# Attention and capacity-limited experts on one core: joined rows of the last tile, an earlier next-to-last scatter, expert counts copied to SBUF with later placements

## The chip, the cores and the metric

One core of one Trainium2 chip. The metric is device time in microseconds of one execution of the whole kernel. A profiled execution gives the trace, from which all rows below come.

## The reference

Causal attention over 8 batches, 12 heads, 448 positions and head width 64; its output, 3584 rows of 768, goes to a top-1 expert layer with 8 experts, at most 80 tokens each (those with the largest gate weight).

```python
scores = scale * np.matmul(q, k.transpose(0, 1, 3, 2))
scores = np.where(mask, -1000000000.0, scores)              # mask: above the diagonal
attn = np.exp(scores - np.max(scores, axis=-1, keepdims=True))
attn = attn / (np.sum(attn, axis=-1, keepdims=True) + 1e-09)
x = np.matmul(attn, v)                                      # then (B*S, H*D): 3584 x 768
...
logits = x @ w_gate
expert_idx = np.argmax(logits, axis=1)
gate_w = probs[np.arange(N), expert_idx]                    # softmax of the logits
for e in range(E):
    tok_idx = np.where(expert_idx == e)[0]
    if len(tok_idx) > capacity:                             # capacity 80
        tok_idx = tok_idx[np.argpartition(-gate_w[tok_idx], capacity)[:capacity]]
    h = np.maximum(x[tok_idx] @ w1[e], 0.0)
    out[tok_idx] = gate_w[tok_idx, None] * (h @ w2[e])
```

## The kernel before

**Attention.** The loop goes over 48 pairs of heads, six per batch, each in 8 slots. The order of instructions on every engine is the order in which the program emits them; nothing reorders it. In one pair's turn TensorE does the corner scores of this pair (L547), transposes the exponentials of the pair before (L597, four groups of four blocks, each in one bank of PSUM out of four that rotate under the tag "g"), multiplies the flipped exponentials of the pair before that with the values (L620), and starts the scores of the next pair (L540). VectorE adds the mask and finds the minimum (L559, `ns`, `nb`), ScalarE takes the exponential (L563), and ScalarE (three groups) and VectorE (the fourth) copy the transposes to the flipped buffer `PT` (L602). The product `xp` is copied to `xu`, one column per query, by ScalarE (L629). The four tiles of 448 queries are three of 128 (t = 0 to 2, queries 64 to 447) and one of 64 (t = 3, the first 64 queries in memory; the code calls it the last tile).

**Steps of a batch.** What a finished batch still needs is spread over the pairs of the next one and a bit further by a table of slots: `later_on` puts a step at `ends` + slot, so slots 0 to 7 fall in pair 0 of the next batch, 16 to 23 in its pair 2, 48 to 55 in pair 0 of the batch after it. `STEPS` has the slots for most batches, `EARLY` those of the next-to-last batch.
- `norms`: `guard`, `invert` and `last_rows` turn the sums of the softmax into their reciprocals; `last_rows` gathers those of the last tile into `rl`.
- `row_group(t, g)`: for tile t and three pairs of heads (g = 0 or 1), three transposes of `xu` (L731), one multiply by the reciprocals (L750), one store to the scratch rows `xs` (L755). `ROWS0` and `ROWS1` have their slots.
- `gate_products` (L681), `gate_rows` and `gate`: logits of the experts.
- `select_groups`: keeps a table of the 80 largest weights of each expert over the batches so far. `rl`, `lt`, `cp` count how many of a batch's tokens are larger than each kept one (`cp`, L908, a bank of PSUM), `places` and `places2` (L928, VectorE, half the experts each) turn the counts into one-hot rows `rm`, `c0` to `c3` compare tokens with each other (L879, L882), `earlier` (GpSimd, `rank`, L968), `own`, `rank` and `rr` make the new tokens' places, `tn` (L1015, L1021) moves the table.

**Tail.** The last batch has no later pair to hide in; its steps stand in the string `TAIL`, which is executed from left to right: `r0w`, `r0e`, `r0m` are the transposes, the copy and the scaling of row group 0 and so on; an engine letter in `ROW_ENGINES` says who scales it ("p": ScalarE copies and GpSimd scales, "a": ScalarE scales). `*25` is 25 matmuls on constants (L1313) whose result nobody reads; they stand between the new table (`tn tab`) and the first expert.

**Experts.** `plan_experts` simulates the engines with a table of costs and returns an order of all steps. TensorE's own order is fixed in it: layer 1 and 2 of the experts alternate, one chunk of 128 inputs at a time ("p"), with "xtp" (transposes of gathered rows, L1374) and "ytp" (transposes of an expert's output, L1478) placed between chunks. `yo` scales the transposed output (L1488, L1490) and GpSimd scatters it to `out` by an indirect DMA (L1491); each scatter waits for the landing of the one before. The first three gathers (L1358) are issued before the first expert, and need the rows stored to `xs`.

Of the kernel before, what the change touches and what calls it, by code (L numbers as in the profile page):

```python
# [17 lines left out]
P = 128  # L18
# [9 lines left out]
ROWS0 = [(2, 2), (3, 4), (9, 9), (19, 20)]  # L28
ROWS1 = [(27, 28), (35, 36), (36, 38), (40, 41)]
STEPS = {'gp': 20, 'gs': 22, 'lp': 24, 'lg': 25, 'logit': 26, 'shifted': 27, 'chosen': 32, 'sums': 33, 'one_hot': 33, 'columns': 33, 'weight': 35, 'weighted': 36, 'parts': 37, 'r0t': 41, 'r0c': 42, 'r1t': 42, 'r1c': 43, 'rl': 44, 'lt': 46, 'c3w': 49, 'c3l': 50, 'cp': 53, 'ro': 53, 'places': 54, 'c2w': 56, 'c2l': 57, 'places2': 54, 'c1w': 58, 'c1l': 59, 'c0w': 60, 'c0l': 61, 'earlier': 61, 'gt': 65, 'own': 67, 'rank': 67, 'rr': 68, 'tn': 73, 'tab': 74, 'rp': 76, 'row': 78}  # L30
# [23 lines left out]
def plan_experts(E, layers, blocks, order, whole, pieces, loaded, buffers, his, los, ready_h, ready_l):  # L54

    pe = [("xtp", 0), ("warm", 0)]
    for e, w in layers:
        for x, c in enumerate(order[e, w]):
            n = len(order[e, w])
            if w == 1 and x == n // 2 and e == 0 and E > 1:  # L60
                pe.append(("xtp", 1))
            if x == (n // 2 if w == 1 else 3) and (e >= 2 if w == 1 else e == E - 1 and e > 0):
                pe.append(("ytp", e - 2 if w == 1 else e - 1))
            if w == 2 and x == n // 2 and e + 2 < E:
                pe.append(("xtp", e + 2))
            pe.append(("p", e, w, c))
# [107 lines left out]
def attention_then_moe(  # L174
# [91 lines left out]
    def whole_tile(t):  # L266

        return slice(queries(t).start, queries(t).start + P)
# [23 lines left out]
    for t in flipped:  # L292
        nc.vector.memset(part_of(t, slice(QB, P), COL[0], [WPT, 2], [COL[1] - COL[0], 2], [1, QB]), 0.0)
        nc.vector.memset(part_of(t, slice(0, QB), COL[2], [WPT, 2], [COL[3] - COL[2], 2], [1, QB]), 0.0)
# [274 lines left out]
    def transpose_groups(pr, n):  # L569

        pr.PT = flipped[n % 2]

        full = lambda t, j, at: pr.P[:, OFF[t, j] + at * QB:OFF[t, j] + at * QB + P]
# [6 lines left out]
        ways = [  # L580
            [(slice(0, P), 0, [[256, 2], [1, 256]], COL[0] + QB, [[WPT, 2], [1, 256]])],
            [(slice(0, P), 0, [[256, 2], [1, 256]], COL[1] + QB, [[WPT, 2], [1, 256]])],
            [(slice(0, P), 0, [[256, 2], [P, 2], [1, P]], COL[0] + S - P,
              [[WPT, 2], [COL[3] - P - (COL[0] + S - P), 2], [1, P]])],
            [(hi, QB, [[256, 2], [P, 2], [1, QB]], COL[2], [[COL[3] - COL[2], 2], [WPT, 2], [1, QB]]),
             (lo, QB, [[P, 2], [1, QB]], COL[1], [[WPT, 2], [1, QB]]),
             (lo, 256, [[QB, 2], [1, QB]], COL[0], [[WPT, 2], [1, QB]])],
        ]
# [46 lines left out]
    def norms(bt, ps):  # L635
# [28 lines left out]
        return [guard, invert, last_rows]  # L664

    def norm_of(bt, t, hs, m):
        return bt.rl[0:m, hs] if t == NO else bt.sums[0:m, t * H + hs.start:t * H + hs.stop]

    def gate_products(bt, which):
# [3 lines left out]
        def products(js=(0, 1), whole=range(NT)):  # L675
            if 0 in js:
                got[:] = [bank([P, len(which) * P], F32, "gp")]
            for x, i in enumerate(which):
                for j in js:
                    for t in whole:  # L680
                        nc.tensor.matmul(got[0][t * 4 * E:(t + 1) * 4 * E, x * P:(x + 1) * P], wgd[:, 2 * i + j, :],  # L681
                                         bt.xu[:, 2 * i + j, whole_tile(t)], start=(j == 0), stop=(j == 1))
# [33 lines left out]
    def row_group(bt, t, g, how="v"):  # L716

        b = bt.b
        m = min(P, S - t * P)
        got = []  # L720

        def turn():
# [7 lines left out]
            for i in range(NH):  # L730
                nc.tensor.transpose(tp[:, i, :], bt.xu[:, g * NH + i, whole_tile(t)], ident)  # L731

        def store():
# [5 lines left out]
            src = tp[0:m].rearrange("k p (j d) -> k (p j) d", d=DH)  # L739
            dst = xr[0:m].rearrange("k (h d) -> k h d", d=DH)  # L740
            norm = norm_of(bt, t, slice(g * 2 * NH, (g + 1) * 2 * NH), m)
# [7 lines left out]
            else:  # L749
                nc.vector.tensor_tensor(out=dst, in0=src, in1=norm.unsqueeze(2).to_broadcast([m, 2 * NH, DH]), op=ALU.mult)  # L750
            write(xr)

        def write(xr):
            r0 = b * S + queries(t).start
            nc.sync.dma_start(xs[r0:r0 + m, g * NH * P:(g + 1) * NH * P], xr[0:m, :])  # L755

        def scaled():
            _, (xr, dst, norm) = got
            nc.gpsimd.tensor_tensor(out=dst, in0=dst, in1=norm.unsqueeze(2).to_broadcast([m, 2 * NH, DH]), op=ALU.mult)
# [65 lines left out]
    def select_groups(bt):  # L825
# [61 lines left out]
        def table_chunk(s):  # L887
# [222 lines left out]
    def batch_plan(bt):  # L1110
# [4 lines left out]
        for g, rows in enumerate((ROWS0, ROWS1)):  # L1115
            for t in range(NT):
# [197 lines left out]
    for i, x in enumerate(ROW_ENGINES):  # L1314
        g, t = divmod(i, NT)
        steps.update(zip((f"r{i}w", f"r{i}e", f"r{i}m"), row_group(bt, t, g, x)))
# [264 lines left out]
```

## Time and profile before

| | us |
|---|---|
| median of 3 runs (lowest, highest) | 448.84 (448.57, 449.16) |
| profiled execution, its own time | 448.39 |
| its span, first to last instruction | 446.7 |

The span is the profiled time without 1.69 us around the first and the last instruction. A line of the trace gives the engine (PE TensorE, PEld its weight loads, DVE VectorE, ACT ScalarE, POOL GpSimd, SP SyncE), the line of the program, the operation, and what it writes and reads.

### The profile page before, as it was taken

How to read it: one execution, taken by the hardware profiler on the slowest of the kernel's cores; microseconds unless marked ns; L12 is line 12 of the kernel's file. 1: busy time of each engine (PE TensorE's matmuls, PEld its weight loads, DVE VectorE, ACT ScalarE, POOL GpSimd, SP SyncE). 2: the span in 40 equal slices, each digit the busy share in tenths (PEclk: the TensorE clock that was granted, in tenths of full speed). 3: DMA queues.
4: the chain of work that ended last, by engine and by line, in shares of the span. 5: the costliest groups of instructions: out<-in, count | busy, mean ns of one | idle time of the engine just before them, and what ended most of it. 6: DMA issues, size and time to landing. Idle time of an engine off the chain costs nothing. (4 is left out here: it accounts for less than half of the span.)

```text
span 446.7 us, 15791 instructions
## 1 busy us (share of the span) xinstructions
PE 427.3 (96%) x5830; PEld 331.0 (74%) x5830; DVE 383.2 (86%) x1315; ACT 391.3 (88%) x1069; POOL 241.5 (54%) x360
## 2 busy tenths in 40 slices
PE   8899999999999999999999999999899999899993
PEld 3576777777677777767766776765559999899992
DVE  6886698979879997987998889788879999989991
ACT  5999999989889988988989898878878999899971
POOL 7987728538665852856685384512561176415521
PEclk9999999999999999999999999999989999999998
DMA  7486769869686874866774354388479999999501
GB/s 228 140 283 213 237 209 322 256 215 307 233 266 203 290 236 139 306 232 230 243 244 151 98 181 148 135 298 307 161 247 346 401 414 400 397 415 412 229 26 45
DMA packets 47822, 109.95 MB, mean 246 GB/s; under 512 B 5970, under 2 KB 24402, under 8 KB 47104
## 3 DMA queue, kind: packets, MB, share of 16 engines
q1 hardware_dynamic: 46544, 105.20, 67.8%
q0 software_dynamic: 1056, 3.51, 2.4%
q8 instruction: 46, 0.75, 0.7%
q14 instruction: 32, 0.26, 0.2%
q10 hardware_dynamic: 144, 0.23, 0.2%
HBM read 85.35 MB, written 23.99 MB: 245 GB/s over the span
## 5 line engine op out<-in xcount | busy, mean ns | idle before, releaser
L563 ACT ACTIVATE prob<-ns,nb 128x192 f32<-128x192 f32 (+3 forms) x336 | 175.5, 532 | 17.6 <-DVE nb L559 16.1
L559 DVE CUSTOM_DVE_ANT_0 ns<-sp,mask 128x192 f32<-128x192 f32 (+3 forms) x336 | 134.4, 443 | 22.8 <-PE sp L540 21.1
L597 PE MATMUL tp<-ident,prob 128*128 128x128 f32 x768 | 104.4, 276 | 0.1
L1158 DVE SCALAR_TENSOR_TENSOR wl<-wraw,wh 128x768 f16<-128x768 f32 (+1 forms) x99 | 98.4, 1062 | 1.9 <-POOL wl L1507 1.6
L488 POOL TENSOR_TENSOR qk<-qk,qk 128x448 f16<-128x448 f32 x94 | 96.8, 1045 | 4.2 <-DVE qk L516 1.0
L620 PE MATMUL xp<-PT,vt 128*64 128x448 f32 (+3 forms) x768 | 93.6, 386 | 0.4 <-ACT PT L602 0.2
L1152 ACT ACTIVATE wh<-wraw 128x768 f16<-128x768 f32 (+1 forms) x99 | 86.5, 939 | 8.4 <-PE hp L1446 6.0
L597 PEld LDWEIGHTS tp<-ident,prob 128*128 128x128 f32 x768 | 84.2, 141 | 2.4 <-ACT PT L602 0.5
L620 PEld LDWEIGHTS xp<-PT,vt 128*64 128x64 f32 x768 | 50.8, 136 | 45.0 <-issue 24.5
L602 ACT COPY PT<-tp 128x512 f32<-128x512 f32 x144 | 76.3, 589 | 6.3 <-PE tp L597 5.8
L540 PE MATMUL sp<-qk 64*128 64x448 f16 (+2 forms) x864 | 69.2, 299 | 2.1 <-POOL qk L488 1.2
L1447 PEld LDWEIGHTS <-wl 128*128 128x128 f16 x678 | 67.7, 100 | 1.5 <-issue 1.4
L1446 PEld LDWEIGHTS <-wh 128*128 128x128 f16 x678 | 67.7, 100 | 1.1 <-issue 1.0
L1445 PEld LDWEIGHTS <-wh 128*128 128x128 f16 x678 | 68.2, 101 | 0.1
L563 ACT ACTIVATION_READ_ACCUMULATOR prob<-ns,nb 128x1 f32 x336 | 66.1, 197 | 0.0
L1491 POOL DMA_INDIRECT out<-yo,idx x8 | 36.8, 4602 | 51.7 <-ACT yo L1488 46.8
L540 PEld LDWEIGHTS <-qk 64*128 64x128 f16 x864 | 36.7, 95 | 17.4 <-issue 2.5
L602 DVE COPY PT<-tp 64x256 f32<-64x256 f32 x144 | 43.6, 327 | 2.3
L1447 PE MATMUL hp<-xh,wl 128*128 128x80 f16 x336 | 37.8, 202 | 1.4 <-issue 1.4
L1446 PE MATMUL hp<-xl,wh 128*128 128x80 f16 x336 | 37.7, 202 | 0.4 <-DVE xl L1390 0.4
L1445 PE MATMUL hp<-xh,wh 128*128 128x80 f16 x336 | 37.9, 202 | 0.0
L1446 PE MATMUL op<-hl,wh 128*128 128x80 f16 x318 | 36.3, 202 | 0.5 <-issue 0.4
(187 smaller groups left out, 658.9 us busy)
## 6 DMA issues: line engine op xcount, KB each, us to landing
wraw<-w SPq DMA_DIRECT2D x49, 384.0 KB, 8.6
wraw<-w SPq DMA_DIRECT2D x29, 512.0 KB, 9.1
out<-mask SPq DMA_DIRECT2D x56, 192.0 KB, 4.2
qk<-k_t SPq DMA_DIRECT2D x23, 448.0 KB, 4.6
qk<-q_t SPq DMA_DIRECT2D x23, 448.0 KB, 5.7
vt<-v_t SPq DMA_DIRECT2D x24, 384.0 KB, 6.1
xs<-xr SPq DMA_DIRECT2D x42, 192.0 KB, 2.8
wraw<-w SPq DMA_DIRECT2D x24, 256.0 KB, 4.3
```

Of the source, the lines that this page charges most:

```text
L488: sub = lambda e, o, a, b: e.tensor_tensor(out=o, in0=a, in1=b, op=ALU.subtract)
L540: nc.tensor.matmul(pr.sp[t, j], a[rows, p, queries(t)], c[rows, p, FROM[t]:FROM[t] + WIDTH[t]], start=(x == 0), stop=(x == 2))
L559: nc.vector.tensor_tensor_reduce(out=ns, in0=pr.sp[x], in1=m, scale=-1.0 / 8.0, scalar=HUGE, op0=ALU.add, op1=ALU.min, accum_out=nb)
L563: nc.scalar.activation(pr.P[:, OFF[x]:OFF[x] + w], got[0], AF.Exp, bias=got[1], scale=-1.0, accum_out=pr.sums[:, h:h + 1])
L597: nc.tensor.transpose(tp[:, i * P:(i + 1) * P], f, ident)
L602: way(part_of(pr.PT, rows, to, *todims), part_of(got[0], rows, at, *dims))
L620: nc.tensor.matmul(xp[rows, c * P:S], st["vt"][:, c, p * P + j * DH:p * P + (j + 1) * DH], pr.PT[:, j, n0:n0 + w], start=(c == 0), stop=(c ...
L1152: nc.scalar.activation(hi_of[y][:, 0:src.shape[1]], src, AF.Copy, scale=SW)
L1158: nc.vector.scalar_tensor_tensor(out=lo_of[y][:, 0:n], in0=src, scalar=SW, in1=hi_of[y][:, 0:n], op0=ALU.mult, op1=ALU.subtract)
L1445: nc.tensor.matmul(o, wh[:, ws], h[:, c, :], start=begin, stop=False, skip_group_check=True)
L1446: nc.tensor.matmul(o, wh[:, ws], l[:, c, :], start=False, stop=False, skip_group_check=True)
L1447: nc.tensor.matmul(o, wl[:, ws], h[:, c, :], start=False, stop=end, skip_group_check=True)
```

## The change

Five edits in one.
1. Pairs of heads with an even number keep their last tile at columns 384 to 447 of `xu` and not at 0 to 63. The last tile of an even pair and of the odd pair after it then lie side by side, and one transpose of 128 columns turns both. For tile 3 there is one row group in place of two: three transposes, one multiply over 128 partitions by a new array of reciprocals `rc`, and two stores, each of 64 rows with three pieces of 512 bytes a row. `rc` is filled by four more small copies on GpSimd per batch. The layouts of `PT`, of the products and of the gate products follow. In the last batch row group 3 and its steps leave `TAIL`, and row group 7 has the joined form.
2. "ytp" of the next-to-last expert stands before the third chunk of the last layer and not before the fourth.
3. `ro`, which did nothing, copies the counts `cp` to SBUF on ScalarE (all batches but the last), in `STEPS` one slot later; the placements read the copy.
4. In `STEPS`, `places` goes from slot 54 to 62 and `places2` from 54 to 68.
5. The matmuls before the first expert are 28 and not 25.

```diff
-ROWS0 = [(2, 2), (3, 4), (9, 9), (19, 20)]
+ROWS0 = [(2, 2), (3, 4), (9, 9)]
 ROWS1 = [(27, 28), (35, 36), (36, 38), (40, 41)]
...
-STEPS = {..., 'cp': 53, 'ro': 53, 'places': 54, ..., 'places2': 54, ...}
+STEPS = {..., 'cp': 53, 'ro': 54, 'places': 62, ..., 'places2': 68, ...}
...
-lp lg r1m rest rest logit r2w shifted r2e rest chosen rest r3w r3e *4
-sums one_hot columns r0t r0c r4w r4e *1 weight weighted parts hold rl r5w r5e r1t r1c *2 r3m r4m
+lp lg r1m rest rest logit r2w shifted r2e rest chosen rest *4
+sums one_hot columns r0t r0c r4w r4e *1 weight weighted parts hold rl r5w r5e r1t r1c *2 r4m
...
-gt1 c0l gt0 earlier own *5 rank rr tn tab *25
+gt1 c0l gt0 earlier own *5 rank rr tn tab *28
...
-            if x == (n // 2 if w == 1 else 3) and (e >= 2 if w == 1 else e == E - 1 and e > 0):
+            if x == (n // 2 if w == 1 else 2) and (e >= 2 if w == 1 else e == E - 1 and e > 0):
...
+    BEFORE = [QB, 0]
+    HEAD = [S - QB, 0]
+
+    def tile_of(bt, p, t):
+
+        at = p * S + (HEAD[p % 2] if t == NT - 1 else queries(t).start - BEFORE[p % 2])
+        return bt.xu.rearrange("k p s -> k (p s)")[:, at:at + P]
...
+                to = c * P - BEFORE[pr.p % 2] if c else 0
...
-                        xp[rows, c * P:S], st["vt"][:, c, p * P + j * DH:p * P + (j + 1) * DH],
+                        xp[rows, to:to + w], st["vt"][:, c, p * P + j * DH:p * P + (j + 1) * DH],
...
+                bt.rc = spool.tile([P, H // 2], F32, name="rqc", tag="rqc")
...
+            for x in range(2):
+                for j in range(2):
+                    nc.gpsimd.tensor_copy(bt.rc[x * QB:(x + 1) * QB, :].rearrange("k (p j) -> k p j", j=2)[:, :, j],
+                                          bt.sums[j * QB:(j + 1) * QB, n + x:n + NP:2])
...
             for i in range(NH):
-                nc.tensor.transpose(tp[:, i, :], bt.xu[:, g * NH + i, whole_tile(t)], ident)
+                nc.tensor.transpose(tp[:, i, :], tile_of(bt, 2 * i if both else g * NH + i, t), ident)
...
-            norm = norm_of(bt, t, slice(g * 2 * NH, (g + 1) * 2 * NH), m)
+            norm = bt.rc if both else bt.sums[:, t * H + g * 2 * NH:t * H + (g + 1) * 2 * NH]
...
+            for x in range(2):
+                nc.sync.dma_start(xs[r0:r0 + QB, :].rearrange("r (i x d) -> r i x d", x=2, d=P)[:, :, x, :],
+                                  xr[x * QB:(x + 1) * QB, :].rearrange("k (i d) -> k i d", d=P))
...
-                    bt.moves.append((table[s][0], got["cp"], sn))
+                    ro = got["cp"]
+                    if not last:
+                        ro = sm("ro", [SL, E])
+                        nc.scalar.copy(ro[0:sn], got["cp"][0:sn])
+                    bt.moves.append((table[s][0], ro, sn))
...
-            for t in range(NT):
+            for t in range(NT - 1 + g):
                 for at, f in zip(rows[t], row_group(bt, t, g)):
```

## Rows read from the trace of the kernel before

**Rows 1.** The page, part 1: busy us, share of the span, instructions.

```profile
PE 427.3 (96%) x5830; PEld 331.0 (74%) x5830; DVE 383.2 (86%) x1315; ACT 391.3 (88%) x1069; POOL 241.5 (54%) x360
```

**Rows 2.** Busy time in single pairs: stretch, length, then busy us (instructions) by engine.

```profile
16.37:21.56 5.19, 5.19 (x54) 3.63 (x54) 3.96 (x16) 5.19 (x20) 4.74 (x9) 1.00 0.48 126
62.25:68.09 5.84, 5.84 (x62) 4.27 (x60) 5.70 (x31) 5.84 (x20) 4.24 (x7) 1.00 0.93 289
80.25:86.20 5.95, 5.95 (x61) 4.18 (x60) 5.34 (x26) 5.76 (x19) 1.33 (x2) 1.00 0.71 222
194.94:201.47 6.53, 6.18 (x61) 4.18 (x60) 6.02 (x27) 5.48 (x18) 1.20 (x2) 1.00 0.53 173
201.47:208.72 7.25, 7.25 (x117) 5.48 (x115) 5.30 (x25) 6.27 (x20) 6.78 (x9) 1.00 0.77 254
```

**Rows 3.** Timeline of pair 1, sixth batch: start, length, engine, line; idle before.

```profile
194.69 0.99 DVE L928 SCALAR_TENSOR_TENSOR rm<-cp,pnum,slots_e 80x320 bf16<-80x320 f32 x2
...
195.61 0.34 DVE L559 CUSTOM_DVE_ANT_0 ns<-sp,mask 128x192 f32<-128x192 f32 x1
...
197.06 0.55 PE L731 MATMUL rt<-ident,xu 128*128 128x128 f32 x3 [0.35 <-ACT PT L602]
```

**Rows 4.** Timeline of GpSimd at the end.

```profile
426.43 3.18 POOL L1491 DMA_INDIRECT out<-yo,idx  x1 [6.58 <-ACT yo L1488]
436.22 1.13 POOL L1491 DMA_INDIRECT out<-yo,idx  x1 [6.62 <-ACT yo L1488]
442.19 0.91 POOL L1491 DMA_INDIRECT out<-yo,idx  x1 [4.83 <-DMA out<-yo,idx]
```

**Rows 5.** Timeline of ScalarE and of VectorE at the end.

```profile
434.90 1.05 ACT L1488 ACTIVATE yo<-ytp,gws 80x384 f32<-80x384 f32 x2 [1.70 <-PE ytp L1478]
...
433.88 2.69 DVE L1158 SCALAR_TENSOR_TENSOR wl<-wraw,wh 128x768 f16<-128x768 f32 x3
...
439.48 0.61 DVE L1490 TENSOR_SCALAR yo<-ytp,gws 80x384 f32<-80x384 f32 x1 [0.62 <-PE ytp L1478]
```

**Rows 6.** Small operations: a group by form, a timeline row, one line's durations.

```profile
L662 POOL COPY rql<-sums 64x6 f32<-64x6 f32 x14 | 2.6, 185 | 0.4
...
316.09 0.19 ACT L1031 CAST tab<-tn 80x40 bf16<-80x40 f32 x1
...
L928 DVE SCALAR_TENSOR_TENSOR rm<-cp,pnum,slots_e x14: 531/533/546, 117.6 to 322.2; 80x320 bf16<-80x320 f32 x14
```

**Rows 7.** Timeline at the end of pair 1, third batch.

```profile
86.12 0.34 DVE L559 CUSTOM_DVE_ANT_0 ns<-sp,mask 128x192 f32<-128x192 f32 x1
```

**Rows 8.** Timeline of pair 2, sixth batch: the set that goes.

```profile
203.14 0.31 PEld L731 LDWEIGHTS rt<-ident,xu 128*128 128x128 f32 x3
```

**Rows 9.** Timeline before the first expert.

```profile
327.14 1.07 POOL L1358 DMA_INDIRECT xg<-xs,idx  x1 [4.17 <-DVE gws L1083]
...
327.96 3.33 PEld L1313 LDWEIGHTS <-identb 128*128 128x128 bf16 x18 [0.22 <-issue]
...
331.39 0.61 PEld L1374 LDWEIGHTS xtp<-ident,xg 80*128 80x128 f32 x6
```

**Rows 10.** The tile of the gathers: issue to landing.

```profile
DMA to landing us min/median/max: 4.0/6.9/8.4
```

**Rows 11.** Busy time before the first expert; the sixth number is the granted clock.

```profile
326.00:328.00 2.00, 2.00 (x7) 0.79 (x6) 0.70 (x5) 2.00 (x3) 0.86 (x1) 0.51 0.95 301
```

**Rows 12.** Timeline in the last layer: two matmuls, three places apart.

```profile
434.15 0.20 PE L1445 MATMUL hp<-hh,wh 128*128 128x80 f16 x1
...
434.26 0.20 PE L1445 MATMUL hp<-hh,wh 128*128 128x80 f16 x1
```

**Rows 13.** The chain of waits: start, length, what.

```profile
426.43 5.21 DMA out<-yo,idx
...
436.22 5.15 DMA out<-yo,idx
```

**Rows 14.** The line of the stores to `xs`: issue to landing.

```profile
DMA to landing us min/median/max: 1.8/2.3/8.7
```

More of the change, by code (lines that the diff above doesn't have):

```diff
@@ L27 @@
 NORMS = [0, 2, 4]
-ROWS0 = [(2, 2), (3, 4), (9, 9), (19, 20)]
+ROWS0 = [(2, 2), (3, 4), (9, 9)]
 ROWS1 = [(27, 28), (35, 36), (36, 38), (40, 41)]
-STEPS = {'gp': 20, 'gs': 22, 'lp': 24, 'lg': 25, 'logit': 26, 'shifted': 27, 'chosen': 32, 'sums': 33, 'one_hot': 33, 'columns': 33, 'weight': 35, 'weighted': 36, 'parts': 37, 'r0t': 41, 'r0c': 42, 'r1t': 42, 'r1c': 43, 'rl': 44, 'lt': 46, 'c3w': 49, 'c3l': 50, 'cp': 53, 'ro': 53, 'places': 54, 'c2w': 56, 'c2l': 57, 'places2': 54, 'c1w': 58, 'c1l': 59, 'c0w': 60, 'c0l': 61, 'earlier': 61, 'gt': 65, 'own': 67, 'rank': 67, 'rr': 68, 'tn': 73, 'tab': 74, 'rp': 76, 'row': 78}
+STEPS = {'gp': 20, 'gs': 22, 'lp': 24, 'lg': 25, 'logit': 26, 'shifted': 27, 'chosen': 32, 'sums': 33, 'one_hot': 33, 'columns': 33, 'weight': 35, 'weighted': 36, 'parts': 37, 'r0t': 41, 'r0c': 42, 'r1t': 42, 'r1c': 43, 'rl': 44, 'lt': 46, 'c3w': 49, 'c3l': 50, 'cp': 53, 'ro': 54, 'places': 62, 'c2w': 56, 'c2l': 57, 'places2': 68, 'c1w': 58, 'c1l': 59, 'c0w': 60, 'c0l': 61, 'earlier': 61, 'gt': 65, 'own': 67, 'rank': 67, 'rr': 68, 'tn': 73, 'tab': 74, 'rp': 76, 'row': 78}
 EARLY = {'gp': 18, 'gs': 20, 'lp': 24, 'lg': 25, 'logit': 26, 'shifted': 26, 'chosen': 28, 'sums': 29, 'one_hot': 29, 'columns': 29, 'weight': 30, 'weighted': 30, 'parts': 30, 'r0t': 33, 'r0c': 34, 'r1t': 35, 'r1c': 36, 'rl': 36, 'lt': 38, 'c3w': 40, 'c3l': 41, 'c2w': 41, 'c2l': 42, 'c1w': 42, 'c1l': 43, 'cp': 43, 'ro': 43, 'c0w': 44, 'c0l': 45, 'earlier': 45, 'places': 46, 'places2': 46, 'gt': 46, 'own': 47, 'rank': 47, 'rr': 47, 'tn': 49, 'tab': 49, 'rp': 52, 'row': 53}
@@ L264, in queries @@
         return slice(0, QB) if t == NT - 1 else slice(QB + P * t, QB + P * (t + 1))
-    def whole_tile(t):
-        return slice(queries(t).start, queries(t).start + P)
+    BEFORE = [QB, 0]
[3 more added lines that the diff above has]
+        return bt.xu.rearrange("k p s -> k (p s)")[:, at:at + P]
     COL = [0, S, 2 * S - P, 3 * S - 3 * P]
@@ L291, in attention_then_moe @@
         nc.tensor.matmul(idle, corners[0][:, 0, 0, :], corners[0].rearrange("k x p q -> k (x p q)"), start=True, stop=True)
-    for t in flipped:
-        nc.vector.memset(part_of(t, slice(QB, P), COL[0], [WPT, 2], [COL[1] - COL[0], 2], [1, QB]), 0.0)
+    for t, at in zip(flipped, HEAD):
+        nc.vector.memset(part_of(t, slice(QB, P), COL[0] + at, [WPT, 2], [COL[1] - COL[0] - at, 2], [1, QB]), 0.0)
         nc.vector.memset(part_of(t, slice(0, QB), COL[2], [WPT, 2], [COL[3] - COL[2], 2], [1, QB]), 0.0)
@@ L571, in transpose_groups @@
         pr.PT = flipped[n % 2]
+        main, head = COL[0] + QB - BEFORE[n % 2], COL[0] + HEAD[n % 2]
         full = lambda t, j, at: pr.P[:, OFF[t, j] + at * QB:OFF[t, j] + at * QB + P]
@@ L580, in transpose_groups @@
         ways = [
-            [(slice(0, P), 0, [[256, 2], [1, 256]], COL[0] + QB, [[WPT, 2], [1, 256]])],
+            [(slice(0, P), 0, [[256, 2], [1, 256]], main, [[WPT, 2], [1, 256]])],
             [(slice(0, P), 0, [[256, 2], [1, 256]], COL[1] + QB, [[WPT, 2], [1, 256]])],
-            [(slice(0, P), 0, [[256, 2], [P, 2], [1, P]], COL[0] + S - P,
-              [[WPT, 2], [COL[3] - P - (COL[0] + S - P), 2], [1, P]])],
+            [(slice(0, P), 0, [[256, 2], [P, 2], [1, P]], main + 2 * P,
+              [[WPT, 2], [COL[3] - P - (main + 2 * P), 2], [1, P]])],
             [(hi, QB, [[256, 2], [P, 2], [1, QB]], COL[2], [[COL[3] - COL[2], 2], [WPT, 2], [1, QB]]),
              (lo, QB, [[P, 2], [1, QB]], COL[1], [[WPT, 2], [1, QB]]),
-             (lo, 256, [[QB, 2], [1, QB]], COL[0], [[WPT, 2], [1, QB]])],
+             (lo, 256, [[QB, 2], [1, QB]], head, [[WPT, 2], [1, QB]])],
         ]
@@ L663, in last_rows, with products @@
                                bt.sums[j * QB:(j + 1) * QB, n + ps.start:n + ps.stop])
+            for x in range(2):
+                for j in range(2):
+                    nc.gpsimd.tensor_copy(bt.rc[x * QB:(x + 1) * QB, :].rearrange("k (p j) -> k p j", j=2)[:, :, j],
+                                          bt.sums[j * QB:(j + 1) * QB, n + x:n + NP:2])
         return [guard, invert, last_rows]
-    def norm_of(bt, t, hs, m):
-        return bt.rl[0:m, hs] if t == NO else bt.sums[0:m, t * H + hs.start:t * H + hs.stop]
     def gate_products(bt, which):
         got = []
-        def products(js=(0, 1), whole=range(NT)):
+        def products(js=(0, 1)):
             if 0 in js:
@@ L678, in products @@
             for x, i in enumerate(which):
[L679 to L682, printed above, removed]
+                turns = [(j, t) for j in js for t in range(NT) if j or 1 in js or t < NT - 1]
+                for j, t in ([] if 0 in js else [(0, NT - 1)]) + turns:
+                    nc.tensor.matmul(got[0][t * 4 * E:(t + 1) * 4 * E, x * P:(x + 1) * P], wgd[:, 2 * i + j, :],
+                                     tile_of(bt, 2 * i + j, t), start=(j == 0), stop=(j == 1))
         def copy():
@@ L718, in row_group @@
         b = bt.b
-        m = min(P, S - t * P)
+        both = t == NT - 1
         got = []
@@ L754, in write @@
             r0 = b * S + queries(t).start
-            nc.sync.dma_start(xs[r0:r0 + m, g * NH * P:(g + 1) * NH * P], xr[0:m, :])
+            if not both:
+                nc.sync.dma_start(xs[r0:r0 + P, g * NH * P:(g + 1) * NH * P], xr)
+                return
+            for x in range(2):
+                nc.sync.dma_start(xs[r0:r0 + QB, :].rearrange("r (i x d) -> r i x d", x=2, d=P)[:, :, x, :],
+                                  xr[x * QB:(x + 1) * QB, :].rearrange("k (i d) -> k i d", d=P))
         def scaled():
             _, (xr, dst, norm) = got
-            nc.gpsimd.tensor_tensor(out=dst, in0=dst, in1=norm.unsqueeze(2).to_broadcast([m, 2 * NH, DH]), op=ALU.mult)
+            nc.gpsimd.tensor_tensor(out=dst, in0=dst, in1=norm.unsqueeze(2).to_broadcast([P, 2 * NH, DH]), op=ALU.mult)
             write(xr)
@@ L1315, in attention_then_moe @@
         g, t = divmod(i, NT)
+        if i == NT - 1:
+            continue
         steps.update(zip((f"r{i}w", f"r{i}e", f"r{i}m"), row_group(bt, t, g, x)))
```

6 lines of the change are left out of this document (3 added, 3 removed).

## The prediction

> **What bounds the kernel now.** I read the page first. It counts TensorE as busy for 96% of the span, its weight loads for 74%, ScalarE for 88% and VectorE for 86% [rows 1], so no share by itself names the bound.
>
> A busy TensorE need not be a limiting one, so the second view is the busy time within single pairs of the attention, each stretch going from one pair's corner product (L547) to the next. They can be compared, since they differ by known work. A pair with nothing beside the attention lasts 5.19 us, one with two sets of three row transposes 5.84 [rows 2]. That is 0.33 us a set, though VectorE had 1.23 us idle in the shorter one and GpSimd more than a microsecond in the longer: TensorE's order of instructions sets the pace. A later pair 1, which carries the selection of the batch before as well, lasts 5.95 us in the third batch, where no table of places exists yet, and 6.53 from the fourth batch on, with the same 61 matmuls [rows 2]. The timeline shows the 0.58: the two placements (L928) hold VectorE until 195.6, so the first softmax shift starts only then, ScalarE's exponential and its copies of the transposes follow late, and TensorE's next row transposes wait 0.35 us for a bank that such a copy frees [rows 3]. In the third batch TensorE is busy for the whole of that pair [rows 2].
>
> The chain of waits names the end: the last scatter starts at 442.19, after 4.83 us of waiting for the landing of the scatter before it, though its own data were ready at 440.09 [rows 4, 5].
>
> **Transposes joined.** Per batch 0 to 6 one set of three transposes, one multiply of VectorE and its bank go, in pair 2 of the next batch. VectorE has 1.95 us idle in that pair (5.30 busy of 7.25 [rows 2]), so only the TensorE part counts: 7 x 0.33 = -2.3 us. The weight loads leave 1.56 of the plain pair's 5.19 us free [rows 2], which by itself would say that TensorE has room and the term is 0; the added sets that lengthened the pair say otherwise, so I keep 2.3. The Trainium skill has the first reading as its rule (Perfetto Trace Analysis, Identifying the Most-Contended Engine: matmul busy share is a poor measure, the weight loads' share a good one); by it the term would be 0 and the sum 2.3 us less of a gain, and the trace does not agree. The stores stay two per batch, now of three pieces a row; nothing of the attention reads them, so they are hidden there.
>
> **Four more copies on GpSimd** per batch (185 ns each by the copies beside them [rows 6], 0.74 us). GpSimd is busy for 1.20 of the 6.53 us of pair 1 [rows 2], waiting there for VectorE's last comparison before `rank`, and that cover is larger than the copies: 0. Without it the split queries and keys behind them would come 0.74 us later, for pairs that start three pairs on. In the last batch they stand before the clearing of the gather buffers and still end well before the first scaled rows: 0.
>
> **Counts copied, placements later.** The copy is one small ScalarE read of PSUM, as the 0.19 us of L1031 [rows 6]. In pair 0 it follows the copy of `xu`, where ScalarE would wait anyway: 0. The two placements (0.53 each, 14 in all [rows 6]: five batches by the late steps, one early, one in the tail) leave the border of pairs 0 and 1. There the pair should fall to the 5.95 us of the third batch: 5 x -0.58 = -2.9 us.
>
> What is late next: one placement now ends pair 1. In the third batch VectorE, without a placement, starts the next shift at 86.12, 0.08 us before that pair's corner product at 86.20 [rows 2, 7]; with 0.53 in between it starts 0.45 after. In today's pair 1 that lateness is 0.67 (195.61 after 194.94) and the bank comes free at 2.12 (197.06) [rows 3]; 0.22 less of it frees the first bank about 1.90 us into pair 2. TensorE wants it at 1.67, where the removed set stands today (203.14 after 201.47) [rows 8]. So 0.23 of the 0.33 won in pair 2 is given back: 5 x 0.23 = +1.1 us; bounds 0 and 5 x 0.58 (the stall merely moves). The second placement in pair 2 takes the place of the removed multiply: 0.
>
> In the last pair the copy of the counts comes ahead of ScalarE's copy of `gs`, whose bank TensorE's `xp` products take next, with nothing to cover it: +0.2 us.
>
> **Tail.** Three transposes, one copy of ScalarE and one product of GpSimd go, and the short steps of VectorE that follow each other there remain, so I take nothing for them (bounds 0 and -0.5, one set with its copy). The three further warm-up matmuls stand right before the first expert's transposes. The 25 end at 331.29 (the last 18 in 3.33 us, 0.185 each) and the transposes start at 331.39; the gather issued at 327.14 needs at least 4.0 us to land [rows 9, 10], so both end together and 3 x 0.185 lengthens the wait: +0.5 us. The lower bound is 0: the granted clock stood at half (1.2 GHz) in 326 to 328, where only 7 of them began in 2 us [rows 11]; if it stays at 2.4 GHz next time, 28 fit before the landing.
>
> **End.** The transposes of expert 6's output (L1478) move one chunk of 18 matmuls ahead, 18/3 x 0.107 = 0.64 us (three matmuls from 434.15 to 434.26) [rows 12]. ScalarE's scaling, now to 435.95, and the scatter behind it, now at 436.22, come as much earlier: 435.58 [rows 4, 5]. VectorE is still busy to 436.57 [rows 5], and descriptors written beside it took 3.18 us at 426.43, against 0.91 with VectorE idle [rows 4]. At that ratio the scatter's descriptors end near 437.2 instead of 437.35. Landing came 2.0 us after the descriptors for the scatter of 426.43 (5.21 less 3.18) and 4.0 for the next (5.15 less 1.13) [rows 4, 13]. No row says why, so I take the shorter, of the scatter that is otherwise the more hindered: landed at 439.2. The last scatter is then held by its own data, 440.09, plus the 0.27 that the one before needed from data to start: 440.36 instead of 442.19, -1.8 us. If the 4.0 comes again, it is -0.2.
>
> **Sum.** -2.3 - 2.9 + 1.1 + 0.2 + 0.5 - 1.8 = -5.2 us on the profiled execution of 448.39 (446.70 span and 1.69 around it): 443.2. The median of the runs lies 0.45 higher: 443.6. From no change I could tell about 0.2%, 0.9 us.
>
> **Rivals.**
> - *The last scatter goes on waiting.* Descriptors beside a busy VectorE and a 4.0 us landing leave 0.2 of the 1.8: 445.2. For it: this landing took 4.0 in the trace. Against: the scatter before it, under a busier VectorE, took 2.0. Chance 0.22.
> - *The stall only moves* from pair 1 to pair 2, with its whole 0.58: -2.9 + 2.9 in place of +1.1: 445.4. For it: VectorE is full at the end of pair 1. Against: it is idle 1.95 us in pair 2. Chance 0.12.
> - *The transposes are no limit*: the weight loads' free 1.56 us a pair [rows 2] swallow the removed sets, and only they. 443.6 + 2.3 = 445.9. Against: 0.33 us for each added set. Chance 0.03. It is the case of the Trainium skill's rule above.
> - *No price in pair 2 and in the tail*: 443.6 - 1.1 - 0.5 = 442.0, and 441.5 with the tail's three transposes. For it: VectorE's and ScalarE's idle time in pair 2. Against: TensorE waited for exactly such copies in pair 1. Chance 0.2.
> - *Slower.* The two stores of the last joined rows are among the last issued before the gather, near 324, in pieces of a third of the size. The gather of the first expert must see them landed, and every expert follows it. It starts at 327.14 [rows 9], so 3.1 us are free; stores landed after a median of 2.3 us and at worst 8.7 [rows 14]. Above 8.3 us the loss passes the 5.2 won: 448.9 and more (8.7 gives 449.2). Only the worst store of this trace did so, with other traffic than there. Chance 0.03.
>
> My forecast holds 0.40. The range takes in the first three rivals at their bounds, 441.5 to 445.7; its own spread in the likeliest case is 442.9 to 444.3. Faster by over 0.2%: 0.95; within: 0.02; slower: 0.03.
>
> **What would show it.** Pair 2 of the second batch (no placements) shorter by 0.33; pair 1 from the fourth batch on near 5.95 and no wait of the row transposes on ScalarE's copies; a wait of the fourth transposing group in pair 2 near 0.2; the gap between the last warm-up matmul and the first expert's transposes closed, the latter later against the gather's issue; the last scatter released by the copy of its own data, not by a landing. Wrong would be: pairs 2 unchanged, ScalarE as the pace in pair 1, or a gather that waits for stores.

## The result and the profile after

The changed kernel takes 444.33 us (median of 4 runs, 443.42 to 444.75); the kernel before, on the same chip, 448.73. The ratio is 0.9887, 95% interval 0.9865 to 0.9908: faster, 0.7 us short of the predicted 443.6 and inside the range. The profiled execution took 444.59 (span 442.9), 3.8 less than that of before.

The page of the changed kernel, its engines as in [rows 1], with two of the DMA queues:

```profile
PE 424.6 (96%) x5809; PEld 329.6 (74%) x5809; DVE 383.3 (87%) x1308; ACT 392.0 (89%) x1074; POOL 252.4 (57%) x391
...
q8 instruction: 45, 0.74, 0.7%
q14 instruction: 32, 0.26, 0.2%
```

The shares are those of before to a point, but for GpSimd's (54% before). What moved shows in single pairs, by the stretches of [rows 2] (length, busy time of each engine, granted clock, DMA): pair 2 of the third batch, then pairs 1 and 2 of the sixth.

```profile
87.25:94.17 6.92, 6.92 (x114) 5.14 (x112) 4.84 (x24) 6.27 (x20) 6.66 (x9) 1.00 0.94 312
194.22:200.18 5.96, 5.96 (x62) 4.20 (x60) 5.19 (x25) 5.69 (x19) 1.96 (x4) 1.00 0.61 197
200.18:207.27 7.09, 7.08 (x113) 5.21 (x112) 6.14 (x26) 6.19 (x20) 6.77 (x9) 1.00 0.96 323
```

Without a table of places pair 2 is 0.33 us shorter (7.25 before, in the third batch as in the sixth). Pair 1 went from 6.53 to 5.96 and TensorE no longer waits in it. Pair 2 with placements went from 7.25 to 7.09 only. The timeline of that pair 1, to be held against [rows 3]: VectorE starts the shift at once, and the row transposes follow without a wait.

```profile
194.09 0.15 ACT L927 COPY ro<-cp 80x8 f32<-80x8 f32 x1
...
194.24 0.34 DVE L563 CUSTOM_DVE_ANT_0 ns<-sp,mask 128x192 f32<-128x192 f32 x1
...
195.83 0.49 PE L737 MATMUL rt<-ident,xu 128*128 128x128 f32 x3
```

At the end, GpSimd's last two scatters (of before: [rows 4]):

```profile
433.03 1.92 POOL L1508 DMA_INDIRECT out<-yo,idx  x1 [5.83 <-ACT yo L1505]
438.33 0.92 POOL L1508 DMA_INDIRECT out<-yo,idx  x1 [3.39 <-DVE yo L1507]
```

The last one no longer waits for a landing. It starts 1.44 us after TensorE's last product (436.89), where it took 2.75 before (442.19 after 439.44).

The whole difference by stretches of the two traces: start to pair 3 of the first batch, counted from 0, +1.39 (21.56 to 22.95; the expectation below calls it the third pair), the other pairs -4.38, last pair to first gather +0.31 (27.21 to 27.52), gather to TensorE's last product +0.13, from there to the last scatter -1.31; with 0.07 in what remains, -3.8.

### The profile page after: what moved, and what is told of

Its sections match the earlier page's. It is cut to its first block, busy times and chain, and to the rows that moved or that the text cites. A ratio compares the mean times of both kernels' runs of the same rounds, so it can differ in the third digit from the quotient of the medians.

```text
span 442.9 us, 15765 instructions
## 1 busy us (share of the span) xinstructions
PE 424.6 (96%) x5809; PEld 329.6 (74%) x5809; DVE 383.3 (87%) x1308; ACT 392.0 (89%) x1074; POOL 252.4 (57%) x391
## 4 chain that ended last, share of the span: by engine, by line
PE 74%; DMA 15%; DVE 4%; ACT 2%; POOL 2%; issue 1%; POOLq 0%; SPq 0%; DVEq 0%; ACTq 0%
PE xp L626 20%; PE tp L602 19%; DMA wraw<-w 14%; PE sp L544 13%; PE rt L737 4%; PE gp L687 3%; PE sp L551 2%; PE wp L1328 2%; PE hp L1463 1%; PE hp L1462 1%; PE hp L1464 1%; ACT prob L567 1%; POOL qk L492 1%; PE op L1464 1%; PE op L1463 1%
## 5 line engine op out<-in xcount | busy, mean ns | idle before, releaser
L1508 POOL DMA_INDIRECT out<-yo,idx x8 | 38.3, 4790 | 49.0 <-ACT yo L1505 45.6
```

## The experiments

**Each part alone.** First the joined rows without the rest: counts read in PSUM, placements, last output and warm-ups as before.

```diff
-                    ro = got["cp"] ... nc.scalar.copy(ro[0:sn], got["cp"][0:sn])
-'ro': 54, 'places': 62, ... 'places2': 68      x == (n // 2 if w == 1 else 2)      *28
+'ro': 53, 'places': 54, ... 'places2': 54      x == (n // 2 if w == 1 else 3)      *25
```

> The kernel before with the joined rows alone: counts read from PSUM, placements, last outputs and warm-up matmuls as before. If TensorE's order sets the pace and the parts add up, pair 2 of the third to eighth batch goes from 7.25 to 6.92 us (0.33 for the set of three transposes that goes, 7 times in all), pair 1 stays at 6.52 with its wait of 0.35, and the time falls by 2.3 us to about 446.4. If transposes don't matter beside the weight loads' free time, pair 2 stays at 7.25 and the time at 448.7. If the 1.4 us that the first three pairs lost in the changed kernel come from the joined rows (their zeroed columns are the only edit that acts there), the third pair starts at about 22.95 here too and the time falls by only 0.9; if they are chance, it starts near 21.56 in this execution or in others of these kernels without a pattern by edit.

446.18 us, ratio 0.9929 (0.9906 to 0.9952). Third and sixth batch, pairs 2, 1, 2:

```profile
86.67:93.59 6.92, 6.92 (x113) 5.15 (x111) 4.84 (x25) 6.27 (x20) 6.65 (x9) 1.00 0.98 319
194.43:200.96 6.53, 6.19 (x62) 4.18 (x60) 6.02 (x27) 5.49 (x18) 1.97 (x4) 1.00 0.55 176
200.96:207.88 6.92, 6.92 (x114) 5.15 (x112) 4.84 (x24) 6.26 (x20) 6.59 (x9) 1.00 0.94 329
```

All seven pairs 2 lost 0.33, pair 1 kept its wait: the transposes are worth 2.3 us. Pair 3 of the first batch begins at 22.36, between the two values expected, so this execution doesn't settle the start. Two things were not expected: the last pair to the gather is 27.54 here too, and the last scatter is already free of the landing (both below).

Next the copied counts with the later placements, on the kernel before:

```diff
-                    bt.moves.append((table[s][0], got["cp"], sn))
+                    ro = got["cp"]
+                    if not last:
+                        ro = sm("ro", [SL, E]); nc.scalar.copy(ro[0:sn], got["cp"][0:sn])
+                    bt.moves.append((table[s][0], ro, sn))
-'ro': 53, 'places': 54, ... 'places2': 54
+'ro': 54, 'places': 62, ... 'places2': 68
```

> The kernel before with the copied counts and the later placements alone. If the parts add up, pair 1 from the fourth batch on goes from 6.52 to 5.96 us (5 times 0.56), the pair 2 after it pays 0.18 for the late multiply or corner copy and goes from 7.25 to about 7.43, and the time falls by 2.8 - 0.9 = 1.9 us to about 446.8, with the last pair 0.3 longer: 447.1. If the wait of pair 1 only moves, pair 2 grows by 0.56 and the time stays. Here pair 2 still has its fourth set of transposes, so VectorE and TensorE have more to do in it: if the give-back is VectorE's late work and not TensorE's order, 0.18 is the least that it can be and the pair could reach 7.6.

452.06 us, ratio 1.0072 (1.0048 to 1.0095): slower. Pair 1 went to 5.96 as expected, but pair 2 to 8.34, with 0.70 us in which TensorE waits:

```profile
202.89:211.23 8.34, 7.64 (x117) 5.72 (x115) 6.62 (x27) 6.25 (x20) 7.20 (x9) 1.00 0.78 273
```

The timeline of that pair has the place of the wait.

```profile
206.49 1.02 DVE L932 SCALAR_TENSOR_TENSOR rm<-ro,pnum,slots_e 80x320 bf16<-80x320 f32 x1
...
207.44 0.48 DVE L997 TENSOR_TENSOR rr<-gt,slots_t 128x320 bf16<-128x320 f32 x1
...
207.84 0.54 DVE L750 TENSOR_TENSOR xr<-rt,rql 64x384 f32<-64x384 f32 x1
...
208.01 1.51 PE L620 MATMUL xp<-PT,vt 128*64 128x448 f32 x8 [0.69 <-issue]
```

`xp` starts 0.09 after `rr` ends (207.92). If the four banks of PSUM go round in the order of the requests, gt, rt, tp, gp, xp as in the kernel before, `xp` gets the bank of `gt`, and `rr` is its last reader. The second placement now stands ahead of `rr` on VectorE. To tell that from the late copies of VectorE behind them, the next kernel only exchanges the two.

```diff
-... 'places2': 68, ... 'rr': 68
+... 'rr': 68, 'places2': 68      (rr first, then the placement)
```

> The copied counts and later placements alone, on the kernel before (pair 2 of 8.34 us), with the comparison of the ranks put ahead of the second placement on VectorE; what follows both (the fourth set's multiply, the copies of the transposes) stays at its time. If the product with v waits for the comparison, because it takes the PSUM bank that the comparison reads, it starts about 1.0 us sooner in pair 2 (4.1 instead of 5.1 us into the pair) and pair 2 is shortened to 7.8 or 7.9, with the later copies as its next limit. If VectorE's late copies of the transposes are what it waits for, nothing moves: 8.34.

Pair 2 is 7.58 us, shorter than either theory gave, and `xp` starts at 204.90, 4.37 us into the pair instead of 5.12. What stands behind the two on VectorE keeps its order and comes 0.41 sooner:

```profile
200.53:208.11 7.58, 7.57 (x117) 5.53 (x115) 6.21 (x27) 6.25 (x20) 7.20 (x9) 1.00 0.80 284
```
```profile
204.13 0.48 DVE L997 TENSOR_TENSOR rr<-gt,slots_t 128x320 bf16<-128x320 f32 x1
...
204.54 0.61 DVE L932 SCALAR_TENSOR_TENSOR rm<-ro,pnum,slots_e 80x320 bf16<-80x320 f32 x1
...
204.90 1.95 PE L620 MATMUL xp<-PT,vt 128*64 128x448 f32 x16
```

So the wait for `rr` is shown: before the exchange `xp` started ahead of the end of the multiply (208.38) and of VectorE's copies (from 208.41), so it did not wait for those. One execution took 446.16. The second placement still further back:

```diff
-'places2': 68
+'places2': 69      (behind rr, the fourth set's multiply and the copies of the transposes)
```

> The copied counts alone on the kernel before, with the first placement at its later place and the second behind the comparison, the fourth set's multiply and the copies of the transposes. If only work ahead of the comparison and the copies costs, pair 1 is 5.96 and pair 2 between 7.25 and 7.40 (the first placement still delays the first shift), and the time falls by 2.1 to 2.8 us against before, to about 447. If the fourth set leaves pair 2 no room for a placement at all, pair 2 or pair 3 grows by 0.5 us or more.

447.91 us, ratio 0.9963 (0.9942 to 0.9983). Pair 2 is 7.57, above the 7.25 to 7.40 expected, as with the exchange: the second placement costs nothing once `rr` is past. The remaining 0.33 over 7.25 lies ahead of it: `gp` starts 2.92 us into the pair in the exchanged kernel (203.45 after 200.53) and 2.59 in the kernel before (204.06 after 201.47), because the first placement at the end of pair 1 makes the shift and ScalarE's copies late (in the exchanged kernel TensorE waits for such a copy ahead of the set that the change removes and again behind it, 0.10 and 0.18).

**Is it the placements' place, or the copy?** The changed kernel with the copy, but the placements at 54:

```diff
-'places': 62, ... 'places2': 68
+'places': 54, ... 'places2': 54
```

> The changed kernel with the counts copied but both placements back at their old place, between pair 0 and pair 1. If the placements' place on VectorE makes the wait of pair 1, it is back: pair 1 of 6.52 us from the fourth batch on with 0.35 of TensorE idle, pair 2 of 6.92. If it was the bank of the counts that was held too long, the copy alone removes the wait: pair 1 of 5.96.

Pair 1 became 7.14 us, longer than before the change, pair 2 6.92; one execution took 448.82. VectorE now also waits for the copy, which ScalarE does late:

```profile
195.33 0.16 ACT L927 COPY ro<-cp 80x8 f32<-80x8 f32 x1
...
195.52 1.23 DVE L943 SCALAR_TENSOR_TENSOR rm<-ro,pnum,slots_e 80x320 bf16<-80x320 f32 x2 [0.24 <-ACT ro L927]
```

TensorE's row transposes of that pair wait 0.96 us in place of 0.35. The place makes the stall; the copy alone worsens it. And without the copy:

```diff
-                    if not last:
-                        ro = sm("ro", [SL, E])
-                        nc.scalar.copy(ro[0:sn], got["cp"][0:sn])
```

> The changed kernel without the copy of the counts: both placements at their later places read the counts in PSUM, whose bank is then held from pair 0 to pair 2, and three banks instead of four go round for some 13 us in each batch from the fourth on. If the copy matters for the bank, TensorE waits for banks in pairs 1 and 2, 0.2 us or more at each of the four groups of transposes of a pair, 1 to 3 us a batch, 5 to 15 us in all. If three banks are enough, pairs 1 and 2 stay at 5.96 and 7.09.

One execution took 452.62. Pair 1 is 7.61 us with 1.26 of waiting, pair 2 7.14: five batches of 1.7, 8.5 us. The copy pays, as expected if it frees the bank.

```profile
197.96:205.57 7.61, 6.35 (x61) 4.17 (x60) 5.99 (x28) 6.11 (x18) 3.17 (x7) 1.00 0.60 197
```

**A bank more in the changed kernel.** One transpose into a bank that nobody reads:

```diff
+        def turned():
+            tp = bank([P, NH, P], F32, "rt")
+            nc.tensor.transpose(tp[:, 0, :], tile_of(bt, 0, 0), ident)
+        later_on(ends + 19, [turned])
```

> The changed kernel with one transpose more in each pair 2, into a bank of its own that nobody reads, at the place where the removed set stood; VectorE's order is untouched. Theory from the copied counts alone (pair 2 of 8.34 us): the four PSUM banks go round, and with a set of transposes between the products of the places and the product with v, that product gets the bank of the places, which VectorE frees only with the comparison behind the second placement. Then pair 2 from the fourth batch on grows by 0.11 for the transpose and by about 1.0 for the wait (xp would start at 5.1 instead of 3.9 us into the pair), to some 8.1 us, and pair 2 of the second and third batch by 0.11 alone. If it was VectorE's multiply of the fourth set that made the later placement dear, pair 2 grows everywhere by 0.11, to 7.20.

Neither. Pair 2 grew by 0.11, 0.22 and then 0.49 (7.57 and 7.58 in the fourth to seventh batch, 7.20 in the eighth); one execution took 446.89. `xp` started at 205.02, ahead of `rr` at 205.21, so it did not wait for it. An unread bank that is free at once and holds no place in the round would explain that, but no run shows it: that in the kernel before the set's bank, and not something else of the set, gave `xp` the bank of `gt` stays argued. What the run does show is that the next transposes waited 0.16 for a bank of ScalarE's copies, and `gp` came 0.48 later into the pair: with VectorE's order untouched, this request costs 0.38 beside its transpose.

**Placements behind everything.** The changed kernel with both at the end of pair 2:

```diff
-'places': 62, ... 'places2': 68
+'places': 70, ... 'places2': 71
```

> The changed kernel with both placements moved to the end of pair 2, behind the comparison and VectorE's copies of the transposes, where VectorE waits 0.9 us for the next pair's scores. If the 0.18 that pair 2 pays is the late first shift and copies behind the placements, pair 2 goes from 7.09 to 6.92 us (its length with the set gone and the placements still in the pair before), pair 1 stays at 5.96, and the time falls by 5 x 0.17 = 0.9 us to 443.4. If two placements of 1.0 us don't fit in that idle time, the first shift of pair 3 comes late and pair 3 grows by 0.3 to 0.6 us instead: no gain.

443.34 us, ratio 0.9858 (0.9832 to 0.9885); pair 2 6.92 in the fourth to seventh batch and 7.01 in the eighth, pairs 1 and 3 unchanged. The give-back is gone, as the first theory had it:

```profile
199.83:206.75 6.92, 6.92 (x113) 5.15 (x112) 6.19 (x26) 6.26 (x20) 6.59 (x9) 1.00 0.95 307
```

**The end.** The sooner output alone:

```diff
-            if x == (n // 2 if w == 1 else 3) and ...
+            if x == (n // 2 if w == 1 else 2) and ...
```

> The kernel before with the next-to-last expert's output one product sooner, alone. If the last scatter was held by the landing of the one before it, it now starts about 0.8 us after its own data, as in the changed kernel, 1.3 us sooner against the end of TensorE's work than before, and the time falls to about 447.4. If that landing was late by chance in the profiled execution, the time stays at 448.7 and the start of the last scatter against TensorE's end varies. Up to the last three experts all lengths stay as before.

448.70 us, ratio 0.9989 (0.9970 to 1.0008): no gain that can be told. The next-to-last scatter started 0.6 sooner but landed 3.48 us after its descriptors (437.37 to 440.85), and the last one waited again. With the joined rows and the old order of the output, by contrast, it landed 2.06 after (436.25 to 438.31), before the last data (439.01):

```profile
435.13 1.12 POOL L1504 DMA_INDIRECT out<-yo,idx  x1 [6.63 <-ACT yo L1501]
439.80 0.92 POOL L1504 DMA_INDIRECT out<-yo,idx  x1 [3.54 <-DVE yo L1503]
```

The DMA views of the stretch between descriptors and landing tell why: in the kernel before, a packet of the queue that the profile calls instruction stands among the scatter's 64; in the kernel with the joined rows there is none.

```profile
q0 software_dynamic: 64, 0.25, 16.8%
q8 instruction: 1, 0.02, 1.1%
```
```profile
q0 software_dynamic: 64, 0.25, 21.4%
```

In the trace of before that packet (16,384 bytes) runs from 439.01 to 439.95. All but four packets of the scatter are done by 439.07; those four run from 439.94 to 440.91. Queue q8 had 46 such packets for the 11,754 recorded instructions of TensorE (11,660 matmuls and weight loads), one for 255, so I take it for TensorE's instruction list. The joined rows alone took 42 of those instructions away, and their trace has no 46th packet; in the changed kernel it comes at 443.30, after the last instruction. A third kernel, the changed one, gets 60 more, by cutting 15 warm-ups in three:

```diff
-        for _ in range(times):
-            nc.tensor.matmul(wp, identb, before[:, 0:S], start=True, stop=True)
+        few = 15 if times > 20 else 0
+        for w in [S] * (times - few) + [152, 152, 144] * few:
+            nc.tensor.matmul(wp[:, 0:w], identb, before[:, 0:w], start=True, stop=True)
```

> The changed kernel with 15 of its 28 warm-up matmuls cut in three (45 of a third of the columns, the same work): 30 matmuls and 30 weight loads more in TensorE's list, 11,775 instead of 11,715. Theory from the runs so far: TensorE's list comes in packets of 16 KB, one for some 255 instructions (46 packets for 11,754); in the kernel before and in those with its matmul count the 46th was read beside the next-to-last scatter and held four of its packets back for 1.9 us, and the joined rows, with 42 instructions fewer, pushed it behind the end. Then here it falls beside that scatter again, the landing takes 3.5 to 4.0 us after the descriptors instead of 2.07, the last scatter starts 1.4 to 2.0 us after its own data instead of 0.78, and the time is about 0.9 longer (445.2). If the sooner output is what freed the last scatter, it starts 0.78 after its data as in the changed kernel, and the time stays at 444.3.

445.25 us, 0.9914 (0.9890 to 0.9938), but the end is not where it was lost. The packet came at 435.28, ahead of most of the scatter, which landed 2.61 after its descriptors, still before the last data: the last scatter started 1.44 after TensorE's end. The cut warm-ups delayed the first expert instead (5.23 from gather to transposes for 4.81). By the count of instructions I had overshot. The kernel with the additional bank hit what this one missed: seven recorded instructions more put a packet at 437.5, the next-to-last scatter landed 3.79 after its descriptors, and the last one waited for it.

```profile
434.11 1.99 POOL L1512 DMA_INDIRECT out<-yo,idx  x1 [5.76 <-ACT yo L1509]
440.70 0.91 POOL L1512 DMA_INDIRECT out<-yo,idx  x1 [4.60 <-DMA out<-yo,idx]
```

Over all fourteen traces: seven with an instruction packet near that scatter's data have 2.61, 3.05, 3.47, 3.61, 3.65, 3.79 and 4.02 us from descriptors to landing, seven without have 2.03 to 2.07. The seven with it have 11,722 to 11,775 recorded instructions of TensorE, the seven without 11,709 to 11,715. The count alone doesn't place the packet, though: with 11,754 it began 0.44 us before TensorE's last product ended in one kernel and 1.47 in another.

**The warm-ups.** The three taken back:

```diff
-gt1 c0l gt0 earlier own *5 rank rr tn tab *28
+gt1 c0l gt0 earlier own *5 rank rr tn tab *25
```

> The changed kernel with 25 instead of 28 warm-up matmuls before the experts. If the gather of the first tokens lands well before the 28th, the first transposes of the tokens start 3 x 0.185 = 0.56 us sooner after the gather (4.25 instead of 4.81) and the time is 443.8 instead of 444.3. If the three stand in time in which TensorE would wait for the gather, nothing changes. The attention stays as in the changed kernel: pair 1 5.96, pair 2 7.09 us.

444.30 us, 0.9899 (0.9861 to 0.9937): no difference to 444.33. The transposes of the first expert came 4.45 us after the gather, for 4.81. From the gather to TensorE's last product this trace has 111.76 us, less than any other with 25, but that stretch varies by more than the three are worth: 111.76 to 112.39 in the seven traces with 25, 111.27 to 112.43 in the six with 28 whole ones. Transposes that come sooner need not gain either: in the kernel with the late placements the granted clock stayed at 2.4 GHz there, the transposes came 3.27 after the gather, and TensorE then waited 1.21 us for VectorE's split of the tokens:

```profile
327.24 0.58 PE L1391 MATMUL xtp<-ident,xg 80*128 80x80 f32 x6
...
331.42 0.20 PE L1463 MATMUL hp<-xl,wh 128*128 128x80 f16 x1 [1.21 <-DVE xl L1407]
```

From the gather to TensorE's last product that is 112.17 us (108.90 from the transposes on), 112.43 in the changed kernel (107.62 from the transposes on), 112.30 in the kernel before.

**The best version.** Late placements, and the last output scaled by ScalarE alone:

```diff
-                if self.e < E - 1 or i == 0:
+                if True:
                     nc.scalar.mul(to, o, g)
```

> The changed kernel with both placements at the end of pair 2, as in the run before, and the last expert's second half of the output scaled by ScalarE instead of VectorE. The seven other scatters start 0.27 to 0.28 us after ScalarE's output, the last one 0.79 after VectorE's. If the difference is the kind of release (the last scatter waits for two engines, and another wait is worked off behind VectorE's), it starts 0.28 after the second half, which ScalarE can do as soon (0.58 for 0.61 us): 0.5 us gained at the end beside the 0.9 of the placements, a time of 442.9. If 0.79 is what a last scatter costs beside the landing before it, the end stays and the time is that of the run before, 443.3.

442.81 us (442.62 to 443.18), ratio 0.9850 (0.9829 to 0.9871). The last scatter starts 0.28 after ScalarE's second half (436.17), so it is the kind of release:

```profile
434.95 1.22 ACT L1505 ACTIVATE yo<-ytp,gws 80x384 f32<-80x384 f32 x2 [0.92 <-PE ytp L1495]
```
```profile
436.45 0.91 POOL L1508 DMA_INDIRECT out<-yo,idx  x1 [3.06 <-ACT yo L1505]
```

It stands 1.5 us below the changed kernel's median, but each was timed beside its own runs of the kernel before, and the intervals of the two ratios touch; what is shown are the two stretches of the trace, 0.76 us in five pairs and 0.55 at the end.

## Why the prediction was right, and where not

The sum was -5.2. The trace without the start gives -4.38 + 0.31 + 0.13 - 1.31 = -5.25. That the two agree so well is luck: the pairs gained 0.3 more than forecast and the experts' stretch lost 0.4 less, the end gained 0.5 less and the last pair lost 0.1 more. Three of the steps behind the sum were not what I took them for. The range's upper bound, 445.7, also left out the rival of 445.9 that it was said to take in.

- **Transposes, -2.3: right.** 0.33 in each of seven pairs. The Trainium skill (Perfetto Trace Analysis, Identifying the Most-Contended Engine) judges TensorE's headroom by its share of peak FLOP/s and the weight loads' busy share, and not by matmul busy share. Read as room for the sets, the free weight loads would have given 0; with the joined rows alone the trace doesn't agree with that reading. That VectorE's multiply counted for nothing was right for this part alone.
- **Pair 1, -2.9: right** (five times 0.56 to 0.57, -2.8), by the mechanism given: the place of the placements.
- **Give-back, +1.1: right in kind, measured +0.76** (four times 0.17, once 0.08). The wait is where it was looked for: the fourth group of transposes starts 1.85 us into pair 2, behind a copy of ScalarE, and 1.70 with the placements behind everything. But "the second placement in pair 2 takes the place of the removed multiply: 0" hid the largest risk. It held only because the set was gone; with it in place the same two placements made pair 2 1.09 longer and the kernel slower. That the set's bank request does it is argued from the round of the banks. The two parts are not a sum.
- **Copy in the last pair, +0.2: wrong.** With the copy alone the last pair to the gather took 27.20 us, as before (27.21); with the joined rows alone 27.54. What is later is SyncE's last store. These are its issues at the end, first of the copied counts alone, then of the joined rows alone:

```profile
319.26 8.30 SPq L755 DMA_DIRECT2D xs<-xrl  x8
```
```profile
315.39 5.03 SPq L762 DMA_DIRECT2D xs<-xrl  x4
321.50 1.18 SPq L765 DMA_DIRECT2D xs<-xrl  x2
322.77 0.55 SPq L762 DMA_DIRECT2D xs<-xrl  x1
```

  The joined rows need two stores, and the one behind them ends 24.90 us into the last pair (323.32 after 298.42) in place of 24.18 (327.56 after 303.38). GpSimd's long wait ahead of the gather ends 1.54 to 1.63 after that issue in four traces: 0.6 before VectorE's index in the two kernels without joined rows, 0.05 and 0.24 after it in the two with them. Over all traces the last pair to the gather is 27.14 to 27.23 in the five without joined rows and 27.49 to 28.24 in the nine with them. That is the rival "slower", at 0.3 us instead of 5, though no run moved that store alone: I had called it decided only above 8.3 us. The +0.2 of the sum met these +0.31 by luck.
- **Warm-ups, +0.5: met at its place (+0.56), but not shown to be theirs, and worth nothing in the time.** From gather to transposes it took 4.19 to 4.78 us with 25 of them where the granted clock fell to 1.2 GHz there (five traces) and 4.81 to 4.82 with 28 whole ones (two); where it stayed at 2.4 GHz, 3.50 and 3.97 with 25 and 3.27 to 3.35 with 28 (four). So the clock decides more than the count, as the forecast's lower bound had it. "At least 4.0 us to land" was wrong: where the trace has the landing of this gather, it took 3.08 to 3.99.
- **End, -1.8: measured -1.31, and the step failed.** The landing did take 2.06 us after the descriptors, as I chose. "No row says why" was the place to stop: the 4.0 was an instruction packet, and not the sooner output but 42 instructions fewer moved it. In the joined kernel the output's old place does as well. The rest is the start after the last data, 0.79 and not 0.27: the 0.27 came from scatters released by ScalarE.
- **The start, not foreseen: +1.39 in the profiled execution.** No edit is needed for it. The two kernels that differ only in where VectorE does the second placement, from the fourth batch on, have the same code up to there, yet pair 3 of the first batch begins at 21.68 and 23.18. Their pairs 1 and 2 (granted clock last but two):

```profile
10.62:16.50 5.88, 3.96 (x39) 2.66 (x38) 5.45 (x26) 5.45 (x20) 5.63 (x13) 1.00 0.39 147
16.50:21.68 5.18, 5.18 (x53) 3.62 (x54) 3.94 (x16) 5.18 (x19) 4.74 (x9) 1.00 0.47 107
```
```profile
10.38:16.96 6.58, 4.16 (x39) 2.73 (x38) 4.88 (x25) 6.22 (x23) 6.34 (x14) 0.91 0.35 132
16.96:23.18 6.22, 6.22 (x53) 4.66 (x54) 3.94 (x16) 4.67 (x14) 5.77 (x10) 0.82 0.59 175
```

  In fourteen traces it begins between 21.56 and 23.56; in the eight in which the granted clock fell to 1.2 GHz between 15 and 20.5 us, from 22.56 on, in the six without that, by 22.36. The second part is TensorE's wait for GpSimd's split of queries and keys (`qk`) in pair 1: of those six, the three at 21.56 to 21.68 wait 0.50 us, the three at 22.12 to 22.36 wait 1.47. The long wait stands in one of the five traces without joined rows and in seven of the nine with them, so that they favour it is neither shown nor excluded. Why the clock falls in some executions stays open, and whether the other runs had it no trace shows; 1.4 us is twice what the prediction missed by.

## What to carry to other kernels

What an instruction waits for can change when another one goes: here the same placement held up `xp` with the set of transposes that the change removes, and not without it. An instruction that goes takes its PSUM bank request with it, so follow the round of banks before moving a reader. The landing that took twice as long as its neighbour had its cause in the DMA view of that stretch; look there for a foreign packet before promising a gain from starting earlier. Test the parts of a change alone: here one part was slower by 0.7% without the other.

## What the runs showed of the hardware

- Instructions come as DMA packets while the kernel runs (46 on queue q8 before), and one of 16 KB delayed the last four packets of a scatter by 1.8 us (439.07 to 440.91), and with them its landing: the first of the four starts at 439.94, as the instruction packet ends. The Trainium skill (DMA: Bandwidth & Descriptors, Issuing engines are not separate DMA queues) says that transfers started by ScalarE, SyncE or GpSimd run on the same 16 DMA engines and interleave, whoever started them. The trace agrees, and shows it for an instruction packet too.
- A scatter released by ScalarE starts 0.27 to 0.31 us after it, the last scatter released by VectorE 0.79 and by a landing 0.81 to 0.82. The Trainium skill (Perfetto Trace Analysis, Identifying Dependency Chains) says that an instruction that waits for several engines may have further waiting instructions put in front of it. That fits: in the changed kernel GpSimd's queue has one whose wait ends 0.04 us after VectorE's output, and the scatter starts 0.75 later (437.59, 438.33). With ScalarE alone it ends before ScalarE's output. Why the step behind it takes 0.75 stays open.
